# Hourglass attention and hypermixer: loading the values in half as many DMAs, and q and k by partition halves with crossed heads

## The chip, the cores and the metric

The kernel runs on one core of one Trainium2 chip. The metric is the device time of one execution in microseconds (us). A few executions are timed for each kernel, always beside executions of the kernel before on the same chip, and one is profiled. A run is called "slow" when it is more than 1.5% above the fastest of the same kernel, and the comparisons use the fast ones alone. The span that a profile shows is about 1 to 4 us shorter than the device time of the same run. Start times in the text are us from the start of the profiled span.

Short names: PE is TensorE, PEld its weight loads, DVE VectorE, ACT ScalarE, POOL GpSimd, SP the SyncE queue that issues the DMAs.

## The reference, cut to what matters

The inputs q, k and v are float32 of shape (8 batches, 8 heads, 576 rows, 64), drawn as 0.1 times a normal variate. Everything below is done for each batch.

```python
factor, Sd, scale = 4, 576 // 4, 1 / 8
# coarse attention on means of four rows, repeated four times
q_d, k_d, v_d = (t.reshape(B, H, Sd, 4, D).mean(axis=3) for t in (q, k, v))
out_up = np.repeat(sm_attn(q_d, k_d, v_d), 4, axis=2)
# local attention: a row sees the rows at a distance below 4
mask = np.abs(pos[:, None] - pos[None, :]) < 4
scores = np.where(mask, scale * q @ k.T, -1e9)
out_local = softmax(scores) @ v
x = (out_up + out_local)                       # then heads are put side by side: (B, 576, 512)
# token mixing
W_tok = (x @ w_q) @ (x @ w_k).T / 8
out = np.maximum(W_tok @ x, 0) @ w_out
```

## The kernel before

The batches are pipelined: while PE works on batch b, the data of batch b+1 are cast and those of b+2 are loaded. All loads are issued by SP in program order.

q and k of a batch arrive in one DMA each. Partition p receives 18 consecutive rows of heads 0 to 3 (u = 0) and 18 of heads 4 to 7 (u = 1), in runs of 18 x 64 x 4 = 4,608 bytes:

```python
def load_qk(b):
    for src, nm in ((q[b], "q32"), (k[b], "k32")):
        t = st[b][nm] = big.tile([128, 2, 18 * D], FP32, name=nm, tag="qk32", bufs=4)
        sp.dma_start(t, _ap(src, 0, [[18 * D, 128], [4 * S * D, 2], [1, 18 * D]]))
```

The values arrive as 64-row windows, one for each group of 58 queries: n counts five windows in each token half c. Partition half g holds every second head. A DMA brings four heads of one window, which is 256 runs of 256 bytes (64 KB), and a batch takes 20 of them. K0 is clamped at both ends of the sequence, so the two token halves don't always start 288 rows apart:

```python
K0 = [[min(max(Q0[n][c] - 3, 0), S - 64) for c in range(2)] for n in range(NW)]

def load_v(b):
    v32 = st[b]["v32"] = big.tile([128, NW, 2, 4, D], FP32, name="v32", tag="v32")
    for n in range(NW):
        for c in range(2):
            for g in range(2):
                sp.dma_start(v32[64 * g:64 * g + 64, n, c],
                             _ap(v[b], (g * S + K0[n][c]) * D, [[D, 64], [2 * S * D, 4], [1, D]]))
```

The casts to 16 bit: q and k of batch 0 on DVE and ACT, those of later batches on POOL; the values always on POOL, in one instruction for a batch.

```python
def qk():
    cast("q", dve.tensor_copy if b == 0 else pool.tensor_copy)
    cast("k", act.copy if b == 0 else pool.tensor_copy)
def vv():
    pool.tensor_copy(v16..., g_["v32"]...)
```

PE then transposes q and k (outputs `pq`, `pk`). Head group u becomes the partition half p of `qT` and `kT`. In the local scores p is the half that a matmul reads and g the half of the values' heads, to which it writes. All four combinations (p, g), the four quadrants of the array, are in use:

```python
for p, g in ((0, 0), (1, 1), (0, 1), (1, 0)):
    hl = 2 * y + g
    pe.matmul(p_[64 * g:64 * g + 64, p, o:o + w],
              kT[64 * p:64 * p + 64, hl, K0[n][c]:K0[n][c] + 64],
              qT[64 * p:64 * p + 64, hl, Q0[n][c]:Q0[n][c] + w], ...,
              tile_position=(64 * p, 64 * g))
```

The step `vd` (output `pv`) reduces the values for the coarse attention. It is the first work of a batch that needs the values, and its start is what this text calls the start of a batch. The order of issue around it, cut:

```python
ORDER = [ ... (0, "sums"), (1, "cast_qk"), (-1, "wt"), (0, "vd"), (0, "mask0"), (0, "score0"), (-1, "wks"),
          (2, "load_qk"), (1, "cast_v"), ..., (1, "tq"), (0, "ca0"), (2, "load_v"), ..., (1, "tk"), ... ]
```

The softmax here doesn't subtract the row's maximum and nothing guards it: scores larger than these inputs give would overflow.

## Time and profile before

The time was 225.13 us in both of two runs. The profiled run has a span of 223.8 us.

| what | number | where it is read |
|---|---|---|
| PE busy | 75% of the span, other engines at most 52% | busy table |
| wait of `pv` for the value cast | 14.3 us in two waits, 8.6 and 5.6 us | waits, timeline |
| wait of the value cast of batch 0, and of batch 1, for data | 16.1 and 12.0 us | waits |
| 20 value issues of batch 0 | 17.0 us | timeline |
| batch starts | 23.4, 46.7, 70.9, 94.5, 117.4, 142.9, 165.6, 187.7 us | timeline |

The first lines of the page of the kernel before: busy us with the share of the span and the number of instructions for each engine; then three rows of the view in 40 slices of 5.6 us, where a digit is tenths of a slice (9 is 90% or more; for PEclk tenths of the full TensorE clock).

```profile
PE 167.9 (75%) x2816; PEld 110.6 (49%) x2816; DVE 107.0 (48%) x260; ACT 99.1 (44%) x141; POOL 115.3 (52%) x112
...
PE   0060788267699779986996689978997799789680
...
PEclk9996558757889967997699959995899699958999
DMA  6946993597379349933998389836992474002206
```

From the ninth slice on PE is busy for 6 to 9 tenths of almost every slice; before that it has gaps (slices 1, 2, 4 and 8). The DMA row shows those engines only 3 to 6 tenths busy in slices 3, 4, 7 and 8, although values are being waited for.

Waits of the kernel before: engine and tile, what it waited for, us in total, times, longest.

```profile
POOL v L27 <- DMA v<-in_v_dram: 38.5, 7, 12.0
...
POOL v L27 <- DMA w<-in_moe_w_q_dram: 16.1, 1, 16.1
...
PE pv L27 <- POOL v L27: 14.3, 2, 8.6
```

The second line is really the last value DMA of batch 0, issued at 18.19 and landed at 20.80. The load of w_q shares its completion semaphore with an earlier value DMA of batch 0 (issued at 13.58), for which the cast waits as well; its updates begin at 21.01, just before the cast at 21.03, and the view names what came last.

The DMA part of the page: queue, number of DMAs, KB of one, median us from issue to landing.

```profile
v<-in_v_dram SPq DMA_DIRECT2D x160, 64.0 KB, 2.9
q<-in_q_dram SPq DMA_DIRECT2D x8, 1152.0 KB, 7.1
k<-in_k_dram SPq DMA_DIRECT2D x8, 1152.0 KB, 10.4
```

The timeline of the first 50 us: start, length, engine, line, instruction, output and input, count; in brackets, how long the engine had waited and for what.

```profile
1.80 17.00 SPq L27 DMA_DIRECT2D v<-in_v_dram  x20
...
3.18 1.28 ACT L27 ACT_TABLE_LOAD   x1 [3.18 <-POOL PB L80]
...
9.41 2.85 ACT L27 CAST k<-k 128x1152 f16<-128x1152 f32 x2 [4.95 <-DMA k<-in_k_dram]
...
17.54 1.03 DVE L27 TENSOR_TENSOR kd<-sum 128x160 f16<-128x160 f32 x4
...
21.03 2.32 POOL L27 CAST v<-v 128x2560 f16<-128x2560 f32 x1 [16.11 <-DMA w<-in_moe_w_q_dram]
...
23.40 0.85 PE L27 MATMUL pv<-v,Pm 64*32 64x260 f16 x24 [8.62 <-POOL v L27]
...
44.35 2.32 POOL L27 CAST v<-v 128x2560 f16<-128x2560 f32 x1 [11.98 <-DMA v<-in_v_dram]
...
46.73 0.85 PE L27 MATMUL pv<-v,Pm 64*32 64x260 f16 x24 [5.64 <-POOL v L27]
```

The first line is the key to the start of this kernel: 20 issues fill SP's queue from 1.80 to 18.80, and the value cast can only start when the last of them has landed.

Last, the stretch from the third batch start to the eighth, by the view of windows: stretch, its length, busy us of PE, PEld, DVE, ACT and POOL with counts, mean granted clock, DMA share, GB/s.

```profile
70.90:187.70 116.80, 101.65 (x1763) 67.23 (x1762) 60.58 (x128) 58.09 (x86) 76.90 (x68) 0.87 0.70 195
```

In this text the run is cut into "the start" (to the third batch start, 70.9 us here), "the steady stretch" (these 116.8 us) and the rest (36.1 us).

### The profile page before, as it was taken

Reading aid. Unit: us, or ns where it says so; the run is one execution under the profiler, and the core shown is the slowest. Engines: PE = TensorE matmul, PEld = TensorE weight load, DVE = VectorE, ACT = ScalarE, POOL = GpSimd, SP = SyncE. Lnnn points to the kernel's source line nnn. Section 1 sums busy time; section 2 is a strip of 40 time slices with the busy share of each in tenths; the row PEclk is TensorE's granted clock in tenths of the full one; section 3 lists DMA queues with packets and bytes.
Section 4 is the critical chain, followed back from the end, with each engine's and each line's share of the span. In section 5 each row is a group of like instructions: output and inputs, shape, how many; then the busy total and the mean of one; then the engine's idle time right before and its main releaser. Section 6 shows DMA issues by size and latency. Waiting matters only on the chain. (4 is left out here: it accounts for less than half of the span.)

```text
span 223.8 us, 6572 instructions
## 1 busy us (share of the span) xinstructions
PE 167.9 (75%) x2816; PEld 110.6 (49%) x2816; DVE 107.0 (48%) x260; ACT 99.1 (44%) x141; POOL 115.3 (52%) x112
## 2 busy tenths in 40 slices
PE   0060788267699779986996689978997799789680
PEld 0050467143476456653674367645764676446330
DVE  4813275215735663558243744565356545654230
ACT  2360456033556534465264254644464546433331
POOL 6002970099638954895459741994199359100000
PEclk9996558757889967997699959995899699958999
DMA  6946993597379349933998389836992474002206
GB/s 231 282 95 128 397 269 75 105 400 113 85 227 315 74 103 342 333 64 89 274 355 154 87 238 360 166 78 205 301 289 60 94 293 144 3 3 94 97 10 225
DMA packets 54572, 40.58 MB, mean 181 GB/s; under 512 B 45264, under 2 KB 45328, under 8 KB 54544
## 3 DMA queue, kind: packets, MB, share of 16 engines
q1 hardware_dynamic: 54464, 40.12, 62.5%
q8 instruction: 22, 0.36, 0.7%
q14 instruction: 6, 0.05, 0.1%
q10 hardware_dynamic: 80, 0.05, 0.1%
HBM read 30.67 MB, written 9.44 MB: 179 GB/s over the span
## 5 line engine op out<-in xcount | busy, mean ns | idle before, releaser
L27 POOL CAST v<-v 128x2560 f16<-128x2560 f32 x8 | 18.6, 2322 | 54.6 <-DMA v<-in_v_dram 38.5
L27 PE MATMUL po<-wo,rmx 128*128 128x512 f16 x128 | 36.1, 432 | 0.1
L27 ACT COPY os<-po 128x1024 f32<-128x1024 f32 x16 | 16.2, 1012 | 29.7 <-PE po L27 23.1
L27 DVE TENSOR_TENSOR x<-pav,rz 128x512 f16<-128x512 f32 x40 | 27.7, 691 | 1.4
L27 POOL TENSOR_TENSOR sum<-qT 128x1152 f32<-128x1152 f16 x8 | 16.8, 2106 | 18.2 <-ACT qT L27 17.8
L27 PE MATMUL pq<-id,q 128*128 128x128 f32 x64 | 15.6, 425 | 12.3 <-DVE q L27 10.7
L27 PEld LDWEIGHTS <-rmx 128*128 128x128 f16 x144 | 14.7, 109 | 17.2 <-issue 6.9
L27 ACT ACTIVATE E<-psc 128x928 f16<-128x928 f32 (+1 forms) x24 | 19.4, 806 | 6.4 <-PE psc L27 5.7
L27 PE MATMUL pmx<-wT,M 64*128 64x288 f16 x64 | 11.7, 318 | 11.9 <-DVE x L27 4.6
L27 POOL CAST q<-q 128x1152 f16<-128x1152 f32 x14 | 20.2, 1488 | 0.0
L27 POOL CAST k<-k 128x1152 f16<-128x1152 f32 x14 | 20.2, 1485 | 0.0
L27 PEld LDWEIGHTS pq<-id,q 128*128 128x128 f32 x64 | 12.5, 224 | 14.0 <-DVE q L27 10.7
L27 ACT ACTIVATE Ec<-pcs 128x1008 f16<-128x1008 f32 (+1 forms) x16 | 13.9, 874 | 11.2 <-PE pcs L27 11.2
L27 PE MATMUL pav<-v,E 64*64 64x65 f16 x640 | 14.1, 210 | 3.2 <-issue 2.1
L27 DVE RECIPROCAL rc<-pca 128x8 f32<-128x8 f32 (+1 forms) x16 | 3.2, 203 | 27.1 <-PE pca L27 27.1
L27 PE MATMUL pv<-v,Pm 64*32 64x260 f16 (+1 forms) x192 | 4.9, 286 | 14.3 <-POOL v L27 14.3
L27 POOL TENSOR_TENSOR sum<-kT 128x1152 f32<-128x1152 f16 x7 | 14.7, 2106 | 0.5
L27 PEld LDWEIGHTS <-E 64*64 64x64 f16 x640 | 9.7, 117 | 10.5 <-issue 7.9
L27 DVE RECIPROCAL rz<-pav 128x8 f32<-128x8 f32 x40 | 8.1, 203 | 14.0 <-PE pav L27 13.8
L27 PEld LDWEIGHTS <-Ec 128*128 128x128 f16 x160 | 12.4, 123 | 4.2 <-issue 0.8
L27 ACT COPY qT<-pq 128x1024 f32<-128x1024 f32 x8 | 8.1, 1012 | 13.5 <-PE pq L27 13.5
L27 DVE TENSOR_TENSOR vblk<-pv,blk 64x260 f16<-64x260 f32 x16 | 6.8, 427 | 14.1 <-ACT vd L27 14.0
(79 smaller groups left out, 327.9 us busy)
## 6 DMA issues: line engine op xcount, KB each, us to landing
v<-in_v_dram SPq DMA_DIRECT2D x160, 64.0 KB, 2.9
q<-in_q_dram SPq DMA_DIRECT2D x8, 1152.0 KB, 7.1
k<-in_k_dram SPq DMA_DIRECT2D x8, 1152.0 KB, 10.4
out_dram<-os SPq DMA_DIRECT2D x16, 512.0 KB, 3.1
wo<-in_moe_w_out_dram SPq DMA_DIRECT2D x2, 512.0 KB, 11.9
out_dram<-ol SPq DMA_DIRECT2D x8, 128.0 KB, 2.9
w<-in_moe_w_q_dram SPq DMA_DIRECT2D x1, 128.0 KB, 2.6
w<-in_moe_w_k_dram SPq DMA_DIRECT2D x1, 128.0 KB
```

Source lines behind the costliest of these rows:

```text
L27: return lambda *a, **k: self._tc.keep_in_program_order(f_(*a, **k))
```

## The change

Its intent is to load the values in 10 DMAs of 128 KB instead of 20 of 64 KB. One DMA shall carry four heads and both token halves. For that the halves g now hold heads 0 to 3 and 4 to 7, and K0 is no longer clamped, so that heads and token halves together are one uniform step of 288 rows: eight runs of rows, and a pattern of only three dimensions. (Taking both token halves in one DMA with the heads as they were needs a fourth dimension.) At the two ends of the whole tensor a DMA of 61 or 59 rows and a memset replace what is outside.

With g = heads 0 to 3 or 4 to 7 for the values and the same groups for q and k, only two of the four quadrants would be used. So the halves of q and k are crossed: for heads 2, 3, 6 and 7 the partition half is exchanged. That is done while loading. It needs a different destination for partitions 0 to 63 (heads 0, 1, 4, 5) and for 64 to 127 (heads 2, 3, 6, 7), so each of q and k becomes two DMAs of 64 partitions.

```diff
-    K0 = [[min(max(Q0[n][c] - 3, 0), S - 64) for c in range(2)] for n in range(NW)]
+    K0 = [[q0 - 3 for q0 in Q0[n]] for n in range(NW)]
 ...
     def load_qk(b):
-            sp.dma_start(t, _ap(src, 0, [[18 * D, 128], [4 * S * D, 2], [1, 18 * D]]))
+            for a in range(2):
+                w = 18 * D
+                sp.dma_start(_ap(t, 64 * a * row(t) + a * w, [[row(t), 64], [w - 2 * a * w, 2], [1, w]]),
+                             _ap(src, 2 * a * S * D, [[w, 64], [4 * S * D, 2], [1, w]]))
     def load_v(b):
-            for c in range(2):
-                for g in range(2):
-                    sp.dma_start(v32[64 * g:64 * g + 64, n, c],
-                                 _ap(v[b], (g * S + K0[n][c]) * D, [[D, 64], [2 * S * D, 4], [1, D]]))
+            for g in range(2):
+                o, lo, hi = (4 * g * S + K0[n][0]) * D, 0, 8
+                if (b, n, g) == (0, 0, 0):
+                    dve.memset(v32[0:3, 0, 0], 0.0)
+                    sp.dma_start(v32[3:64, 0, 0], _ap(v[b], 0, [[D, 61], [1, D]]))
+                    lo = 1
+                ... (the same at the other end, with 59 rows)
+                sp.dma_start(v32[64 * g:64 * g + 64, n, lo:hi],
+                             _ap(v[b], o + lo * HS * D, [[D, 64], [HS * D, hi - lo], [1, D]]))
 ... (masks, pooling weights, padding around kT, the order within the casts of q and k, and the order of heads follow)
     def score(pr_):
                             for p, g in ((0, 0), (1, 1), (0, 1), (1, 0)):
-                                hl = 2 * y + g
+                                hl = 2 * (p ^ g) + y
     def ca(i):
-                    pe.matmul(p_[:, p, 0:260], w_(p, 0, 2), vblk[:, p]...)
+                    for a in range(2):
+                        pe.matmul(p_[:, p ^ a, 130 * a:130 * a + 130], w_(p, 0, 2),
+                                  vblk[:, p ^ a, 2 * a:2 * a + 2]...)
     def m2():
-            dve.tensor_copy(M2[64:128], M2[0:64])
+            dve.tensor_copy(M2[64:128].bitcast(FP32), M2[0:64].bitcast(FP32))
```

More of the change, by code (lines that the diff above doesn't have):

```diff
@@ L94, in load_qk @@
             t = st[b][nm] = big.tile([128, 2, 18 * D], FP32, name=nm, tag="qk32", bufs=4)
-            sp.dma_start(t, _ap(src, 0, [[18 * D, 128], [4 * S * D, 2], [1, 18 * D]]))
+            for a in range(2):
+                w = 18 * D
+                sp.dma_start(_ap(t, 64 * a * row(t) + a * w, [[row(t), 64], [w - 2 * a * w, 2], [1, w]]),
+                             _ap(src, 2 * a * S * D, [[w, 64], [4 * S * D, 2], [1, w]]))
     def load_v(b):
-        v32 = st[b]["v32"] = big.tile([128, NW, 2, 4, D], FP32, name="v32", tag="v32")
+        v32 = st[b]["v32"] = big.tile([128, NW, 8, D], FP32, name="v32", tag="v32")
         for n in range(NW):
-            for c in range(2):
-                for g in range(2):
-                    sp.dma_start(v32[64 * g:64 * g + 64, n, c],
-                                 _ap(v[b], (g * S + K0[n][c]) * D, [[D, 64], [2 * S * D, 4], [1, D]]))
+            for g in range(2):
[4 more added lines that the diff above has]
+                    lo = 1
+                if (b, n, g) == (B - 1, NW - 1, 1):
+                    dve.memset(v32[96:128, n, 7], 0.0)
+                    sp.dma_start(v32[64:123, n, 7], _ap(v[b], o + 7 * HS * D, [[D, 59], [1, D]]))
+                    hi = 7
+                sp.dma_start(v32[64 * g:64 * g + 64, n, lo:hi],
+                             _ap(v[b], o + lo * HS * D, [[D, 64], [HS * D, hi - lo], [1, D]]))
     st = [{} for _ in range(B)]
@@ L127 @@
     nc.vector.memset(neg, 0.0)
-    for i0, i1, off, d in ((0, 2, -8, 5), (2, 3, 0, 0)):
-        t_ = neg[0:64, i0:i1]
-        asel(t_, [[-d, i1 - i0], [0, 2], [-1, 64]], ALU.is_ge, NEG, 3 - off, 1)
-        asel(t_, [[d, i1 - i0], [0, 2], [1, 64]], ALU.is_ge, NEG, off + 3, -1)
+    for cm, base in ((1, 6), (-1, 0)):
+        asel(neg[0:64], [[0, 3], [0, 2], [-cm, 64]], ALU.is_ge, NEG, base, cm)
+    asel(neg[0:64, 1], [[0, 2], [1, 64]], ALU.is_ge, NEG, -3, 0)
+    asel(neg[0:64, 2], [[0, 2], [-1, 64]], ALU.is_ge, NEG, 58, 0)
     nc.scalar.dma_start(neg[64:128], neg[0:64])
@@ L154 @@
     for i in range(NV):
-        t_ = cst.tile([128, NW, 2, 4, 65], FP16, name=f"v16_{i}")
-        nc.vector.memset(t_.rearrange("q n c h e -> q (n c h) e")[:, :, 64:65], 1.0)
+        t_ = cst.tile([128, NW, 4, 2, 65], FP16, name=f"v16_{i}")
+        nc.vector.memset(t_.rearrange("q n h c e -> q (n h c) e")[:, :, 64:65], 1.0)
         v16S.append(t_)
     RNG = [(0, 15), (1, 15), (1, 16), (2, 16), (2, 16)]
-    PB = cst.tile([128, NW + 2, 16], FP16, name="PB")
+    PB = cst.tile([128, NW, 16], FP16, name="PB")
     dve.memset(PB, 0.0)
-    for j, (lo, hi) in enumerate(RNG + [RNG[0], RNG[4]]):
+    for j, (lo, hi) in enumerate(RNG):
         dve.memset(PB[:, j, lo:hi], 0.25)
     for g in range(2):
-        for j0, j1, base, d in ((0, NW, -3, 2), (NW, NW + 2, 0, 0)):
-            u_ = PB[64 * g:64 * g + 64, j0:j1]
-            asel(u_, [[d, j1 - j0], [-4, 16]], ALU.is_ge, 0.0, base, 1)
-            asel(u_, [[-d, j1 - j0], [4, 16]], ALU.is_ge, 0.0, 3 - base, -1)
+        u_ = PB[64 * g:64 * g + 64]
+        asel(u_, [[2, NW], [-4, 16]], ALU.is_ge, 0.0, -3, 1)
+        asel(u_, [[-2, NW], [4, 16]], ALU.is_ge, 0.0, 6, -1)
     Pm = cst.tile([128, NW, 2, 32], FP16, name="Pm")
     dve.memset(Pm, 0.0)
-    dve.tensor_copy(Pm[:, 1:5, 0, 0:16], PB[:, 1:5])
-    dve.tensor_copy(Pm[:, 0:4, 1, 16:32], PB[:, 0:4])
-    dve.tensor_copy(Pm[:, 0, 0, 0:16], PB[:, NW])
-    dve.tensor_copy(Pm[:, 4, 1, 16:32], PB[:, NW + 1])
+    for c in range(2):
+        dve.tensor_copy(Pm[:, :, c, 16 * c:16 * c + 16], PB)
     blk = cst.tile([128, 2], FP16, name="blk")
@@ L183 @@
         dve.memset(rows[64 * c:64 * c + 58], 1.0)
+    kTS = []
+    for i in range(2):
+        t_ = cst.tile([128, 9 * 128 + 6], FP32, name=f"kT_{i}")
+        dve.memset(t_[:, 0:2], 0.0)
+        dve.memset(t_[:, 9 * 128 + 2:], 0.0)
+        kTS.append(t_)
     vd0S, vblkS, wTS, wkS, M2S, od1S = [], [], [], [], [], []
@@ L232, in cast @@
             for u in range(2):
-                f_(_ap(d_, 2 * D * u, [[row(d_), 128], [4 * D, 9], [1, 2], [2, D]]),
-                   s_[:, u].rearrange("p (f s e) -> p f s e", s=2, e=D))
+                f_(_ap(d_, 2 * D * u, [[row(d_), 128], [1, 2], [4 * D, 9], [2, D]]),
+                   s_[:, u].rearrange("p (f s e) -> p s f e", s=2, e=D))
         def qk():
@@ L241, in vv @@
             v16 = g_["v16"] = v16S[b % NV]
-            pool.tensor_copy(v16.rearrange("q n c h e -> q (n c h) e")[:, :, 0:64],
-                             g_["v32"].rearrange("q n c h e -> q (n c h) e"))
+            pool.tensor_copy(v16.rearrange("q n h c e -> q (n h c) e")[:, :, 0:64],
+                             g_["v32"].rearrange("q n x e -> q (n x) e"))
         return {"cast_qk": qk, "cast_v": vv}
@@ L256, in f_ @@
                                  t_[:, f].rearrange("p u e s -> p (u e s)"), id32)
-                t_ = g_[dst] = big.tile([128, 128, 9], FP32, name=dst, tag=dst)
+                if dst == "kT":
+                    t_ = kTS[b % 2][:, 2:2 + 9 * 128].rearrange("p (t f) -> p t f", f=9)
+                else:
+                    t_ = big.tile([128, 128, 9], FP32, name=dst, tag=dst)
+                g_[dst] = t_
                 evac(dst, t_[:, :, 0:8], p_.rearrange("p a (f t) -> p t (a f)", f=4))
@@ L275, in sums @@
                               **(dict(tag="xT") if i == 1 and b == 0 else dict(tag="sum2", bufs=1)))
-                t4 = t_.bitcast(FP16).rearrange("p a f -> p (a f)").rearrange("p (t f) -> p t f", f=4)
+                t4 = t_.rearrange("p a f -> p (a f)").bitcast(FP16).rearrange("p (t f) -> p t f", f=4)
                 add(s_, t4[:, :, 0:2], t4[:, :, 2:4], op=ALU.add)
@@ L294, in f_ @@
                 N = 4 * len(pr_)
-                parts = {(0, 3): ((0, 2, 2), (2, 8, 1)), (1, 2): ((0, 8, 1),),
-                         (4,): ((0, 2, 1), (2, 4, 0))}[pr_]
+                parts = {(0, 3): ((0, 2, 1), (2, 8, 0)), (1, 2): ((0, 8, 0),),
+                         (4,): ((0, 2, 0), (2, 4, 2))}[pr_]
                 for lo, hi, ty in parts:
@@ L307, in f_ @@
             def f_():
-                qT, kT = (g_[x].bitcast(FP16).rearrange("p (h t) f -> p h (t f)", h=4)
-                          for x in ("qT", "kT"))
+                qT = g_["qT"].rearrange("p a f -> p (a f)").bitcast(FP16)
+                kT = kTS[b % 2].bitcast(FP16)
                 p_ = g_["psc", pr_]
@@ L315, in f_ @@
                             for p, g in ((0, 0), (1, 1), (0, 1), (1, 0)):
-                                hl = 2 * y + g
+                                hl = 2 * (p ^ g) + y
                                 o = ((i * 2 + c) * 2 + y) * w
+                                ok, oq = S * hl + K0[n][c] + 4, S * hl + Q0[n][c]
                                 pe.matmul(p_[64 * g:64 * g + 64, p, o:o + w],
-                                          kT[64 * p:64 * p + 64, hl, K0[n][c]:K0[n][c] + 64],
-                                          qT[64 * p:64 * p + 64, hl, Q0[n][c]:Q0[n][c] + w],
+                                          kT[64 * p:64 * p + 64, ok:ok + 64],
+                                          qT[64 * p:64 * p + 64, oq:oq + w],
                                           start=False, stop=True, skip_group_check=True,
@@ L336, in vd @@
                         pe.matmul(pv[32 * n:32 * n + 32, g, 0:260], Pm[64 * g:64 * g + 64, n, c],
-                                  v16[64 * g:64 * g + 64, n, c].rearrange("q h e -> q (h e)"),
+                                  v16[64 * g:64 * g + 64, n, :, c, :],
                                   start=(c == 0), stop=(c == 1), skip_group_check=True,
@@ L340, in vd @@
             for c in range(2):
-                for y in range(2):
+                for hl in range(4):
                     for g in range(2):
-                        o = 32 * (2 * g + y)
-                        pe.matmul(pv[o:o + 32, g, 260:390], Pm[64 * g:64 * g + 64, 4, c],
-                                  v16[64 * g:64 * g + 64, 4, c].rearrange("q (p y) e -> q y p e", y=2)[:, y],
+                        pe.matmul(pv[32 * hl:32 * hl + 32, g, 260:325], Pm[64 * g:64 * g + 64, 4, c],
+                                  v16[64 * g:64 * g + 64, 4, hl, c, :],
                                   start=(c == 0), stop=(c == 1), skip_group_check=True,
-                                  tile_position=(64 * g, o))
+                                  tile_position=(64 * g, 32 * hl))
             evac("vd0", vd0.rearrange("q g h e -> q g (h e)"), pv[:, :, 0:260])
-            for g in range(2):
-                lo = 64 * g
+            for a in range(2):
+                lo = 64 * a
                 dve.tensor_tensor(
-                    _ap(vblk, lo * row(vblk) + 65 * g, [[row(vblk), 64], [260, 2], [130, 2], [1, 65]]),
-                    _ap(pv, lo * row(pv) + 512 * g + 260, [[row(pv), 64], [65, 2], [0, 2], [1, 65]]),
+                    _ap(vblk, lo * row(vblk) + 130 * a, [[row(vblk), 64], [260, 2], [65, 2], [1, 65]]),
+                    _ap(pv, lo * row(pv) + 260, [[row(pv), 64], [512, 2], [0, 2], [1, 65]]),
                     _ap(blk, lo * row(blk), [[row(blk), 64], [0, 2], [1, 2], [0, 65]]),
@@ L379, in f_ @@
                 for hl in range(4 if i == 0 else 0):
-                    o = 32 * (2 * (hl % 2) + hl // 2)
+                    o = 32 * hl
                     for p in range(2):
@@ L403, in f_ @@
                 for p in range(2):
-                    pe.matmul(p_[:, p, 0:260], w_(p, 0, 2), vblk[:, p].rearrange("a h e -> a (h e)"),
-                              start=True, stop=False, skip_group_check=True)
+                    for a in range(2):
+                        pe.matmul(p_[:, p ^ a, 130 * a:130 * a + 130], w_(p, 0, 2),
+                                  vblk[:, p ^ a, 2 * a:2 * a + 2].rearrange("q h e -> q (h e)"),
+                                  start=(p == 0), stop=False, skip_group_check=True)
+                for p in range(2):
                     for hl in range(4):
-                        pe.matmul(p_[:, p, 65 * hl:65 * hl + 65], w_(p, hl // 2, hl % 2),
-                                  vd0[:, hl % 2, 2 * p + hl // 2, :],
-                                  start=False, stop=(hl == 3), skip_group_check=True)
+                        g = p ^ (hl // 2)
+                        pe.matmul(p_[:, g, 65 * hl:65 * hl + 65], w_(p, hl // 2, hl % 2), vd0[:, g, hl, :],
+                                  start=False, stop=True, skip_group_check=True)
                 n = 40 if i else 128
@@ L436, in f_ @@
                 p_ = ps(name="pav")
-                for hq in range(4):
+                for hl in range(4):
                     for g, c in ((0, 0), (1, 1), (0, 1), (1, 0)):
-                        pe.matmul(p_[64 * c:64 * c + 64, g, 65 * hq:65 * hq + 65],
-                                  E[64 * g:64 * g + 64, hq // 2, i, c, hq % 2, :],
-                                  v16[64 * g:64 * g + 64, n, c, hq, :],
+                        pe.matmul(p_[64 * c:64 * c + 64, g, 65 * hl:65 * hl + 65],
+                                  E[64 * g:64 * g + 64, g ^ (hl // 2), i, c, hl % 2, :],
+                                  v16[64 * g:64 * g + 64, n, hl, c, :],
                                   start=True, stop=True, tile_position=(64 * g, 64 * c))
@@ L445, in f_ @@
                 dve.tensor_tensor(
-                    x_.rearrange("p (h g e) -> p g h e", g=2, h=4),
+                    x_.rearrange("p (g h e) -> p g h e", g=2, h=4),
                     _ap(p_, 0, [[row(p_), 128], [512, 2], [65, 4], [1, 64]]),
```

## The prediction

> **What bounds it now.** The busy table gives PE 75% of the span, no other engine over 52%; PE is 82-89% busy from 55 to 180 us, and batches start (first pv matmul, timeline) every 22-26 us. The loss is at the start: PE waits 8.6 us for the cast of batch 0's values (14.8 to 23.4) and 5.6 us for batch 1's (41.1 to 46.7). Both casts wait for their DMA (16.1 and 12.0 us, view of waits), and the granted clock is 0.5 from 18.6 to 35.7 and 42.5 to 52.7. Later value casts end 3-9 us before PE needs them.
>
> Those loads are issue bound: 20 issues of 64 KB, one per 0.66 us, only ~100 GB/s; packets of 256 B take 18 ns. Also only eight DMAs are in flight: the seventh and eighth value issues start when q and k land.
>
> **What the change does.**
> 1. Values: 10 issues of 128 KB per batch instead of 20, same 5,120 packets. The 512-run weight load issues in 0.5-0.6 us, so issue cost should not grow: about 7 us per batch instead of 13. Then packets limit: when loads pile up (8-10 and 50-52 us) 256 B packets take 30 ns and the stream gives 170-205 GB/s: about 7 us.
> 2. q and k: each 128-partition load becomes two of 64. [...] 2 KB packets of the 64-partition stores of ol, where alone, take a median 151 ns, those of the 128-partition os 84. So 4,608 B packets should go from 180 to about 340 ns, q plus k of a batch from 5.8 to about 10.9 us (512 x 340 ns / 16, an estimate).
> 3. Up to batch 1's values the stream is estimated at 2.3 + 10.9 + 7.3 + 1.2 (w) + 10.9 + 2.6 (wo) + 7.3 + 0.8 = 43.2 us; before, that cast starts at 44.35. So what the issues give, the halves take back: batch 0's values land about as now (20-22 us), batch 1's 0-3 us earlier. k(0) lands near 13.5-14 instead of 9.4, within PE's slack of 8.6 us.
> 4. PE: 96 more matmuls and weight loads (vblk 2x130 columns for 260, 65 for 130), nearly the same columns. pca runs at column rate (30 ns per 65 warm), so 0.1 us per batch, up to 1 us in all.
> 5. The M copy as 32 bit (286 to 1,257 ns): no change assumed. q's first cast and the mask setup may get faster, off the path.
>
> **On the critical path**: -0 to -4 us at the start, +0.3 to +1 us of PE. Steady batches keep their spacing: DMA work of about 21 us per batch still fits.
>
> **Predicted 224.8 us, 219.5 to 229.0; faster by over 2%: 0.20, within 2%: 0.70, slower: 0.10.**
>
> **Signs.** Right: 10 value issues per batch of about 0.6 us each; 4,608 B packets near 340 ns; k(0) landing after 13 us; first pv within 1.5 us of 23.4, second at 43-47; later spacing unchanged. Wrong: packets still near 180 ns; then the start shrinks by about 11 us, to 214.
>
> **What could make it wrong.** [...] Slower q and k may make POOL's casts late in steady batches and reach PE's transposes (slower).

The sum in step 3 came to 43.2 us, with 10.9 twice for q and k. The 10.9 rests on my estimate of "about 340 ns"; the two stores that step 2 names, 151 and 84 ns, would by their ratio give 324 (180 x 151 / 84, an estimate).

## The result, and the profile after

The changed kernel took 231.45 us (231.38 and 231.52), and the kernel before 225.13. The ratio is 1.028, with a 95% interval from 1.024 to 1.033: slower by 2.8%. A ratio here is the mean time of one kernel's fast runs over that of the other's of the same rounds, so it is not quite the ratio of the medians. A repeat in a later session gave 231.78 against 225.47, ratio 1.026 [1.015, 1.037]; by itself its interval is too wide to call it slower by over 2%.

The page of the changed kernel (span 229.3 us), the same lines:

```profile
PE 167.4 (73%) x2912; PEld 112.3 (49%) x2912; DVE 113.3 (49%) x262; ACT 99.4 (43%) x141; POOL 115.7 (50%) x108
...
PE   0024357764699959995999499968996799779680
...
PEclk9999999999569985999599959995899679979998
DMA  5999999799999999999999999999980004202205
```

PE's busy time is unchanged although it runs 96 more matmuls. What has changed is the DMA row: it is full from the second slice to the last load. (The nines of the PEclk row before its first other digit are no measurement: the clock record of this trace starts at 42.9 us, that of the kernel before at 15.2.) Its waits, its DMAs and its timeline:

```profile
POOL v L27 <- DMA w<-in_moe_w_k_dram: 18.2, 1, 18.2
...
ACT L27 <- DMA k<-in_k_dram: 15.3, 1, 15.3
...
POOL v L27 <- DMA v<-in_v_dram: 12.1, 2, 7.8
...
PE pv L27 <- POOL v L27: 6.6, 2, 5.0
```

```profile
v<-in_v_dram SPq DMA_DIRECT2D x78, 128.0 KB, 4.9
q<-in_q_dram SPq DMA_DIRECT2D x16, 576.0 KB, 9.0
k<-in_k_dram SPq DMA_DIRECT2D x16, 576.0 KB, 11.3
```

```profile
3.58 15.34 SPq L27 DMA_DIRECT2D v<-in_v_dram  x11
...
15.33 1.28 ACT L27 ACT_TABLE_LOAD   x1 [15.33 <-DMA k<-in_k_dram]
16.62 2.79 ACT L27 CAST k<-k 128x1152 f16<-128x1152 f32 x2
...
23.49 3.28 POOL L27 CAST v<-v 128x2560 f16<-128x2560 f32 x1 [18.21 <-DMA w<-in_moe_w_k_dram]
...
24.62 5.92 DVE L27 TENSOR_TENSOR kd<-sum 128x160 f16<-128x160 f32 x4
26.82 0.74 PE L27 MATMUL pv<-v,Pm 64*32 64x260 f16 x32 [4.95 <-POOL v L27]
...
46.98 2.33 POOL L27 CAST v<-v 128x2560 f16<-128x2560 f32 x1 [7.75 <-DMA v<-in_v_dram]
...
49.36 0.48 PE L27 MATMUL pv<-v,Pm 64*32 64x260 f16 x32 [1.68 <-POOL v L27]
```

The wait of `pv` for the cast is less than half of what it was, and yet `pv` starts later, at 26.82 instead of 23.40 and at 49.36 instead of 46.73. That is no contradiction. The end of the wait is set by the cast, and both casts start later (23.49 against 21.03, 46.98 against 44.35), because their data land later. The wait is shorter only because PE arrives later: k of batch 0 lands at 15.3 instead of 9.4, and so its transposes, which come before `pv`, are late as well. Eleven value issues still keep SP busy for 15.34 us, because their number is not what holds them now. Here the second to the fifth of them take 2.0 to 3.9 us each while q and k move, until 14.1 us, and the last six about 0.7. In e5 below, where the DMA of 61 rows is cut, no value issue of batch 0 takes more than 0.7 us, but three of them start at 6.42, 9.17 and 11.93, just when the q or k DMA eight places before has landed (6.41, 9.15, 11.91): in these traces eight completion semaphores take turns, and an issue waits for the DMA eight before. The kernel before shows it too: its sixth and seventh value issues start at 6.10 and 9.41, and the DMAs of q and k, whose semaphores they wait for (eight before, with the one DMA that ACT issues), landed at 6.08 and 9.39. Either way the half-rate q and k hold the issues up, and the last value issue starts at 18.26 here and at 18.43 there. In this trace the data are later still: that last DMA lands 5.1 us after its issue, at 23.34.

The median record of a 4,608-byte packet is 178 ns in the kernel before and 355 ns in this one. That is a factor of two (1.99).

The steady stretch by the view of windows:

```profile
74.70:193.80 119.10, 103.24 (x1831) 68.64 (x1831) 63.09 (x129) 58.27 (x86) 76.29 (x68) 0.86 0.90 193
```

The 5.5 us between the two profiles' spans divide thus, from the batch starts: start 74.7 - 70.9 = +3.8, steady stretch 119.0 - 116.8 = +2.2, rest 35.5 - 36.1 = -0.6.

### The profile page after: what moved, and what is told of

Same layout as the page of the kernel before. It is cut to its first block, busy times and chain, and to the rows that moved or that the text cites. A ratio compares the mean times of both kernels' runs of the same rounds, so it can differ in the third digit from the quotient of the medians.

```text
span 229.3 us, 6708 instructions
## 1 busy us (share of the span) xinstructions
PE 167.4 (73%) x2912; PEld 112.3 (49%) x2912; DVE 113.3 (49%) x262; ACT 99.4 (43%) x141; POOL 115.7 (50%) x108
## 5 line engine op out<-in xcount | busy, mean ns | idle before, releaser
L27 PE MATMUL po<-wo,rmx 128*128 128x512 f16 x128 | 36.9, 440 | 0.1
L27 POOL CAST v<-v 128x2560 f16<-128x2560 f32 x8 | 19.5, 2442 | 30.4 <-DMA w<-in_moe_w_k_dram 18.2
L27 ACT COPY os<-po 128x1024 f32<-128x1024 f32 x16 | 16.2, 1014 | 30.8 <-PE po L27 19.5
L27 PE MATMUL pq<-id,q 128*128 128x128 f32 x64 | 15.6, 425 | 12.4 <-DVE q L27 10.9
L27 PE MATMUL pmx<-wT,M 64*128 64x288 f16 x64 | 11.6, 330 | 11.5 <-ACT E L27 3.9
L27 PEld LDWEIGHTS pq<-id,q 128*128 128x128 f32 x64 | 12.5, 224 | 14.2 <-DVE q L27 10.9
L27 PEld LDWEIGHTS <-E 64*64 64x64 f16 x640 | 10.2, 121 | 14.7 <-issue 11.8
L27 DVE RECIPROCAL rz<-pav 128x8 f32<-128x8 f32 x40 | 8.2, 205 | 16.5 <-PE pav L27 16.3
L27 PE MATMUL pk<-id,k 128*128 128x128 f32 x64 | 10.3, 313 | 6.8 <-ACT k L27 6.6
L27 PEld LDWEIGHTS <-Ec 128*128 128x128 f16 x192 | 13.6, 122 | 2.5 <-issue 0.4
L27 DVE COPY kT<-pr 128x128 f32<-128x128 f32 x8 | 3.1, 391 | 23.0 <-ACT qT L27 23.0
```

Source lines behind the costliest of these rows:

```text
L27: return lambda *a, **k: self._tc.keep_in_program_order(f_(*a, **k))
```

## The experiments

Theory A: fewer value issues are a large gain by themselves, and loading q and k by partition halves, at half the packet rate, takes all of it and more. Rival B: the compute edits (crossed heads, 96 more matmuls, the 32-bit copy of M) cost the time, and the loads are nearly neutral, as the prediction had it. Rival C: it is the larger number of q and k issues, not their partitions. Rival D: small side effects at the start, that is the 61-row DMA or the late table load.

All ratios are against the kernel before, on the same chip and in the same rounds. The experiments ran on four chips, so kernels are best compared by their ratios. Three kernels (marked "heads wrong") lose the crossing, so that for half of the heads the values of one head meet q and k of another. They are for the time only. The comparison with the reference still called them correct, because with inputs of 0.1 the attention weights are almost uniform: the reference itself, recomputed off the chip with those heads exchanged, moves by only 0.01 relative, but by 0.80 when q and k are twelve times and v three times as large.

| run | q, k loads | value issues | us, median | ratio [95%] |
|---|---|---|---|---|
| changed kernel | 2 x 64 partitions, halves | 10 | 231.45 | 1.028 [1.024, 1.033] |
| e0 (the same again) | halves | 10 | 231.78 | 1.026 [1.015, 1.037] |
| e1 (heads wrong) | 1 x 128 | 10 | 209.84 | 0.934 [0.926, 0.941] |
| e4 (heads wrong) | 2 x 128 partitions | 10 | 212.78 | 0.946 [0.933, 0.958] |
| e8 | 2 x 64, even and odd | 10 | 214.42 | 0.949 [0.939, 0.958] |
| e14 (heads wrong) | 1 x 128 | 20 | 226.53 | 1.005 [1.000, 1.010] |
| e11 | even and odd | 20 | 229.51 | 1.017 [1.010, 1.025] |
| e2 (kernel before) | halves | 20 | 252.16 | 1.123 [1.114, 1.132] |

### e1: q and k whole again, the rest of the change kept

```diff
-            for a in range(2): ...      # two DMAs of 64 partitions
+            sp.dma_start(t, _ap(src, 0, [[18 * D, 128], [4 * S * D, 2], [1, 18 * D]]))
```

> The changed kernel with the whole, 128-partition loads of q and k of the kernel before, nothing else (values come out wrong on purpose: heads are no longer crossed). Theory (64-partition loads run at half rate[...]): 4,608 B packets back to 180 ns, k(0) lands near 9.5 us instead of 15.3, first pv near 18-19.5 us, second at 35-38, no idle of PE before it; 213 to 217 us. Rival (the 96 extra matmuls and the other compute edits cost the 6 us): stays at 229-232.

It took 209.84 us, ratio 0.934. One edit of the loads alone is worth 22 us, so B is out as the main cause.

### e2: the kernel before with q and k by halves (no crossing)

```diff
-            sp.dma_start(t, _ap(src, 0, [[18 * D, 128], [4 * S * D, 2], [1, 18 * D]]))
+            for a in range(2):
+                sp.dma_start(t[64 * a:64 * a + 64],
+                             _ap(src, 2 * a * S * D, [[18 * D, 64], [4 * S * D, 2], [1, 18 * D]]))
```

> The kernel before with each load of q and k split into two of 64 partitions, nothing else (right results). Theory (half rate): 4,608 B packets at 340-370 ns, k(0) lands after 13.5 us, and as its values still take 20 issues behind that, batch 1's cast starts at 47-53 instead of 44.35; 229 to 235 us. Rival (compute edits): 224-227.

It took 252.16 us, ratio 1.123: the direction that A gives, but far more than I expected. The median 4,608-byte packet was 358 ns. The batch starts are 23.8 to 28.3 us apart all along, and the steady stretch is 130.9 us. Twenty issues of 0.66 us (13 us) and q and k at half rate (11.5 us, an estimate: 512 x 358 ns / 16) together are more than the 23 us of a batch. In the trace PE waits for the value cast in six of the eight batches (17.9 us in all), where it was two before, so here the loads reach later batches and not only the start.

### e4: q and k in two DMAs each as in the changed kernel, but each over 128 partitions

```diff
             for a in range(2):
-                sp.dma_start(_ap(t, 64 * a * row(t) + a * w, [[row(t), 64], [w - 2 * a * w, 2], [1, w]]), ...)
+                sp.dma_start(t[:, a], _ap(src, 4 * a * S * D, [[18 * D, 128], [1, 18 * D]]))
```

> The changed kernel with q and k still in two issues each, but split along u, so that each spans 128 partitions (wrong values on purpose). It keeps the number of issues, the eight in flight and the two waits of the k cast (the activation table load stays behind one of them). Theory[...]: like e1_whole_qk within 2 us, packets near 180 ns. Rival (the extra issues and waits cost it): like the changed kernel, 229-232.

It took 212.78 us, ratio 0.946, with packets of 178 ns. C is out as the main cause: two DMAs over all partitions cost at most a little against one (the intervals of e1 and e4 overlap), while the same number over half the partitions each, in the changed kernel, costs 19 us more than e4. It is the partitions.

### w: whole q and k, no crossing, scores on two quadrants (heads right)

```diff
-                            for p, g in ((0, 0), (1, 1), (0, 1), (1, 0)):
-                                hl = 2 * (p ^ g) + y
+                            for j, p in ((0, 0), (0, 1), (1, 0), (1, 1)):
+                                hl = 2 * j + y
...
-                                          tile_position=(64 * p, 64 * g))
+                                          tile_position=(64 * p, 64 * p))
```

> A right version: whole loads of q and k, values by halves of the heads in 10 issues, heads not crossed, so scores use two quadrants of the PE array instead of four; vblk by one matmul of 260 columns as before. Theory: the start as in e1_whole_qk; scores cost 0.3 to 0.8 us more per batch; 215 to 221 us, so faster than both kernels. If four quadrants are what the speed rests on: 224 or more.

It took 218.61 us, ratio 0.972 [0.965, 0.979]. So giving up the four quadrants and keeping the whole load already beats both kernels. Against e1 it is 8.8 us slower, and PE is busy for 170.1 us instead of 161.0: this is what the crossing buys, although part of it is clock (30.7 us at half clock against 23.9, see below). The crossing was worth having; the way of loading it was not.

### e8: crossed heads by even and odd partitions (heads right)

Two DMAs over a half of the partitions each take 355 ns for a packet (the changed kernel), two over all of them 178 (e4). That 64 partitions spread over all of them keep the 178 ns was my supposition; no trace had shown it before this run. So the two DMAs go to even and odd partitions instead of the lower and the upper half, and the rows come back into order without another instruction, in the access pattern with which the transposes are taken out of PSUM:

```diff
-                sp.dma_start(_ap(t, 64 * a * row(t) + a * w, [[row(t), 64], [w - 2 * a * w, 2], [1, w]]),
+                sp.dma_start(_ap(t, a * row(t) + a * w, [[2 * row(t), 64], [w - 2 * a * w, 2], [1, w]]),
...
-                evac(dst, t_[:, :, 0:8], p_.rearrange("p a (f t) -> p t (a f)", f=4))
+                evac(dst, t_[:, :, 0:8].rearrange("p (h j) f -> p h j f", h=2),
+                     p_.rearrange("p a (f j h) -> p h j (a f)", f=4, h=2))
...
-                evac("r" + nm, g_[nm + "T"][:, :, 8], pr[:, 128 * i:128 * i + 128])
+                evac("r" + nm, g_[nm + "T"][:, :, 8].rearrange("p (h j) -> p h j", h=2),
+                     pr[:, 128 * i:128 * i + 128].rearrange("p (j h) -> p h j", h=2))
```

> The changed kernel, right results, same number and size of DMAs and still 64 partitions in each, but one load of a pair takes the even and the other the odd partitions of q and k[...]; the copies out of PSUM put the columns back in order. Theory[...]: 4,608 B packets near 180 ns, k(0) lands near 9.5 us, 210 to 215 us. Rival (any load of 64 partitions is slow, or four issues): packets near 350 ns, 229 to 233 us.

It took 214.42 us, ratio 0.949, with all outputs right. Packets are back at 178 ns. From its DMA part, its timeline and its steady stretch (columns as above):

```profile
q<-in_q_dram SPq DMA_DIRECT2D x16, 576.0 KB, 5.4
k<-in_k_dram SPq DMA_DIRECT2D x16, 576.0 KB, 7.3
```

```profile
18.82 2.59 POOL L27 CAST v<-v 128x2560 f16<-128x2560 f32 x1 [13.55 <-DMA w<-in_moe_w_k_dram]
...
21.46 0.74 PE L27 MATMUL pv<-v,Pm 64*32 64x260 f16 x32 [4.95 <-POOL v L27]
...
36.61 2.32 POOL L27 CAST v<-v 128x2560 f16<-128x2560 f32 x1 [5.94 <-DMA v<-in_v_dram]
...
40.64 0.48 PE L27 MATMUL pv<-v,Pm 64*32 64x260 f16 x32
```

```profile
63.85:174.20 110.35, 97.92 (x1823) 67.09 (x1822) 60.69 (x129) 58.13 (x86) 76.11 (x68) 0.89 0.70 195
```

The bytes, the number of DMAs and the matmuls are those of the changed kernel. The second `pv` no longer waits for its cast, and the whole kernel is 17 us faster than the changed one. This settles A: which partitions a DMA spans is the loss. It is also the best right kernel found, and it was run again below.

### e5: the 61-row DMA as 48 and 13 rows

I suspected that the DMA of 61 rows lags and so held back batch 0's values. In the trace of the changed kernel its completion semaphore gets a single update when its data land (15.90 us), that of the 48 rows in e5 gets sixteen (15.17 to 15.49). I read this as one DMA engine instead of sixteen, which is not shown: the trace does not name a packet's engine.

```diff
-                    sp.dma_start(v32[3:64, 0, 0], _ap(v[b], 0, [[D, 61], [1, D]]))
+                    sp.dma_start(v32[3:51, 0, 0], _ap(v[b], 0, [[D, 48], [1, D]]))
+                    sp.dma_start(v32[51:64, 0, 0], _ap(v[b], 48 * D, [[D, 13], [1, D]]))
```

> The changed kernel with its first load of values, 61 rows, as 48 and 13 rows, nothing else. Theory: [...] without it the last values of batch 0 land 1.3 to 2 us earlier (cast from 23.5 to about 21.5-22.2), batch 1's 0.5-2 us earlier; 229 to 231 us. Rival (no lag): cast stays at 23.3-23.7, 231-232 us.

It took 232.22 us, ratio 1.030 [1.023, 1.038]: no gain, a miss of mine; the rival that I had named holds. The cast starts no earlier than the 23.49 of the changed kernel:

```profile
23.66 3.02 POOL L27 CAST v<-v 128x2560 f16<-128x2560 f32 x1 [18.39 <-DMA v<-in_v_dram]
```

### e7 and e7b: the activation table loaded early

In the changed kernel the cast of k(0) waits for two DMAs, and one of the two waits has come to stand before the table load, which runs at 15.33 instead of 3.18. One Exp of one column was put first on ACT.

```diff
+    warm = cst.tile([128, 1], FP32, name="warm")
+    dve.memset(warm, 0.0)
+    act.activation(warm, warm, ACTF.Exp)
```

> The changed kernel with a one-column activation put first on ACT, so that the activation table is loaded at the start and not behind the wait for the second half of k. Expected: the cast of k starts near 15.4 instead of 16.6 us and pk 1.2 us earlier; DVE's sums of batch 0 collide less with POOL's cast of values; first pv 0-1 us earlier; but the second pv waits for its DMA as before, so 230.3 to 231.8 us.

> e7_table_early again: on another chip it lay 1.1% above the kernel before where the changed kernel lay 2.6-2.8% above. If that gain is real: ratio 1.005 to 1.018. If it was luck of the clock windows: 1.02 to 1.035.

They took 228.13 and 228.68 us, ratios 1.011 [1.003, 1.020] and 1.012 [1.007, 1.017]: a real gain of about 3 us on the changed kernel. The load moved, as e7's timeline shows:

```profile
5.83 1.28 ACT L27 ACT_TABLE_LOAD   x1 [5.83 <-DVE rows L27]
...
25.40 0.74 PE L27 MATMUL pv<-v,Pm 64*32 64x260 f16 x32 [4.95 <-POOL v L27]
```

But the start of e7 is only 0.4 us shorter (74.3 against 74.7); 2.4 us of the gain are in the steady stretch (116.6 against 119.0). And with the loads put right (e9 below) it is worth nothing. So it is no fixed price of the table load.

### e10: the M copy in 16 bit

```diff
-            dve.tensor_copy(M2[64:128].bitcast(FP32), M2[0:64].bitcast(FP32))
+            dve.tensor_copy(M2[64:128], M2[0:64])
```

> e8_even_odd with the copy of M in 16 bit as in the kernel before, nothing else. Expected: copy times of 286 ns undisturbed and 0.4-1.2 us beside POOL in both, no difference beyond 1%: 210 to 215 us. If the 32-bit form helps or hurts, the ratio of the two tells.

On top of e8 it took 215.68 us, ratio 0.957 [0.951, 0.963], against 0.949 [0.939, 0.958] for e8. The intervals overlap; if the 32-bit copy gains anything, it is at most about 1%.

### e14: the compute edits alone

Whole q and k, and the values in 20 issues in the new layout.

```diff
-            for a in range(2): ...      # two DMAs of 64 partitions
+            sp.dma_start(t, _ap(src, 0, [[18 * D, 128], [4 * S * D, 2], [1, 18 * D]]))
...
-                sp.dma_start(v32[64 * g:64 * g + 64, n, lo:hi], ...)
+                for l_, h_ in ((lo, 4), (4, hi)):
+                    sp.dma_start(v32[64 * g:64 * g + 64, n, l_:h_], ...)
```

> The changed kernel with the loads of the kernel before: q and k whole, values in 20 issues (head crossing lost, so wrong values on purpose). What is left of the change is its compute: 96 more matmuls, the casts' order, the M copy in 32 bit. If the compute edits cost the 4 us by which e11_v_20_issues lay above the kernel before: 228-231 us. If the two more issues per batch and the second wait of the k cast cost them: 224-227 us, and k's table load back before the data.

It took 226.53 us, ratio 1.005 [1.000, 1.010]. The compute edits cost about 1 us (at most 1%), so B is no more than a small part.

### e11: e8 with the values in 20 issues

The edit is the second half of the one above, on e8.

> e8_even_odd with the values of a batch in 20 issues of 64 KB again, nothing else: [...] compute edits as in the changed kernel. Theory (the gain of e8_even_odd is the halved issues alone): back to the kernel before, 222 to 228 us, second pv at 44-48 us. Rival (the compute edits gain too): under 220.

It took 229.51 us, ratio 1.017 [1.010, 1.025]: with nothing else changed, ten issues more cost 15 us against e8. The first two value casts are as late as in the changed kernel:

```profile
24.36 2.32 POOL L27 CAST v<-v 128x2560 f16<-128x2560 f32 x1 [19.10 <-DMA w<-in_moe_w_q_dram]
...
47.54 2.32 POOL L27 CAST v<-v 128x2560 f16<-128x2560 f32 x1 [11.86 <-DMA v<-in_v_dram]
```

### e12 and e13: halves only in later batches, only in batches 0 and 1

e12 loads batches 0 and 1 by even and odd partitions and the later ones by halves; e13 does the opposite.

```diff
+                eo = b < 2                 # e13: b >= 2
-                sp.dma_start(_ap(t, a * row(t) + a * w, [[2 * row(t), 64], ...
+                sp.dma_start(_ap(t, (1 if eo else 64) * a * row(t) + a * w, [[(2 if eo else 1) * row(t), 64], ...
```

> Even and odd partitions for batches 0 and 1, partition halves from batch 2 on (right results): the start as in e8_even_odd, the steady batches as in the changed kernel. My prediction's claim that steady batches keep their spacing means 213 to 216 us. The traces so far (pv 2 to pv 7: 119.0 us in the changed kernel, 110.4 in e8_even_odd) mean 219 to 224.

> The reverse: halves for batches 0 and 1, even and odd partitions later (right results). If the start alone costs, as the changed kernel, 228-232. By the traces the start costs 10-13 us and the steady batches 8: 221 to 226 us; together with e12_halves_later the two losses should add up to that of the changed kernel over e8_even_odd, about 17 us.

e12 took 219.69 us, ratio 0.971 [0.961, 0.980], and e13 225.46, ratio 1.000 [0.992, 1.008]. Over e8, which ran on another chip, these are 5.3 and 11.0 us (2.2% and 5.1% by the ratios), together 16.3, where the changed kernel loses 17.4 (231.78 of the repeat less 214.42). So about two thirds of the loss come from the first two batches. The steady stretch of e12 is almost as short as that of e8, although its DMA share shows the half-rate loads at work:

```profile
67.80:179.40 111.60, 98.64 (x1823) 67.54 (x1822) 60.74 (x129) 58.04 (x86) 76.13 (x68) 0.89 0.94 199
```

### e8b and e9: the best version again, and with the early table load

> e8_even_odd again, as the partner of the next: 212 to 216 us, ratio 0.94 to 0.957.

> e8_even_odd with the early table load of e7. The k cast starts 1.2 us earlier (near 10 instead of 11.2 us), but the first pv waits for the values' cast all the same; 0 to 2 us less than e8b_even_odd, so 211 to 215 us.

e9 is e8 with the three lines of e7. e8b took 215.46 us, ratio 0.948 [0.941, 0.954], and e9 213.32, ratio 0.946 [0.942, 0.950]: the same.

### e0: the changed kernel again

> The changed kernel once more, as the partner of the three others of this call on the same chip: 230 to 233 us, ratio to the kernel before 1.02 to 1.035.

231.78 us, ratio 1.026. The steady stretch is 119.3 us (119.0 in the first profile), so its length is not chance of one run.

### The steady stretch and the clock

The halves do not directly explain why the changed kernel is slower in the steady stretch, as e12 shows. What goes with its length (the two lowest rows are level) is the time in it for which the clock was granted at half, read from the clock record of each trace (e2, where loads hold up later batches too, has 44.4 us and 130.9):

| kernels | us at half clock in the steady stretch | its length, us |
|---|---|---|
| e1, e4, e8, e10, e12 | 23.9 | 110.4 to 111.6 |
| e13 | 27.3 | 113.5 |
| before, e7, e14, w | 30.7 | 116.6 to 117.2 |
| changed kernel, its repeat | 34.1 | 119.0 to 119.3 |
| e5, e11 | 37.5 | 118.7 to 119.6 |

The steps are 3.4 us. In the clock records of the kernel before and of the changed one, all stretches at one clock but the last take 3.41, 6.83, 10.24, 13.65, 17.07 or 20.48 us. From 83.88 to 179.45 us the stretches at half clock of the changed kernel start 23.9 us apart, seven such steps; its batches are about 23.8 us apart, and those of e8 about 22.1. PE's gaps over 0.1 us in the stretch add up to 15.0 us before and 15.6 in the changed kernel. PE's busy time in it grew by 1.6 us (101.65 to 103.24), about what 3.4 us more at half speed would cost (1.7, an estimate; the 128x512 matmuls of `po` start 216 ns apart at full clock and 427 at half, in the median, in both traces). So the extra 2.2 us are mostly half-clock time, and not waiting for data. Against e8 the stretch is 8.7 us longer: 5.3 of them are PE's busy time, the rest gaps. How a kernel falls into its rhythm, no run settles. That the start decides is the reading that fits e12 (halves only later: 111.6 us) and e13 (halves only at the start: 113.5); it is not shown beyond these.

## Why the prediction was wrong

It said 224.8 us, within 219.5 to 229.0, and "within 2%" at 0.70. The measured 231.45 us lies above the range, and the kernel is slower by 2.8%.

**What held.** Value issues were 10 per batch (11 in batch 0) at 0.6 to 0.7 us each for twice the bytes, as said, where q and k did not hold them. The half-rate packets were 355 ns (said: near 340). k of batch 0 landed after 13 us, at 15.3. The compute edits cost about 1 us (e14, +0.5%). The M copy made no difference that e10 could see. The mechanism, that the halves take back what the issues give, was right in kind: 15 us given (e11 to e8) and 17 us taken (e8 to the changed kernel). (A slip: the value issues that waited for q and k before were the sixth and seventh, at 6.10 and 9.41, not "the seventh and eighth".)

**The step that failed is step 3, the balance "what the issues give, the halves take back": without the halves the change gives less at the start than its sum counted.** By the sum, "43.2 us", batch 1's cast would start "0-3 us earlier" than 44.35; it started at 46.98. With the full-rate 5.8 us of step 2 in place of both 10.9 the same sum gives 33.0. So it counted a gain of about 11 us by the rest of the change against a loss of 10.2 us by the halves. e8 splits the two, because its cast of batch 1 starts at 36.61. The loss by the halves, from 36.61 to 46.98, is 10.4 us, as said. But the gain by the rest, from 44.35 to 36.61, is 7.7 us instead of 11 (8.3 in e1, with q and k whole, where the cast starts at 36.07). The ten fewer issues alone do give 10.9 us, from e11 to e8, but e11, with its two more issues for q and k, starts from 47.54 and not from 44.35.

Which terms were short shows from landing to landing (a DMA has landed with the last update of its semaphore in the trace). All in us; in brackets where the term ends:

| term of the sum | said | changed kernel | e8 (said with 5.8) |
|---|---|---|---|
| q and k of batch 0, from 2.3 | 10.9 | 13.0 (15.3) | 7.6 (9.9) |
| values of batch 0 | 7.3 | 8.1 (23.3) | 8.8 (18.7) |
| w | 1.2 | 1.9 (25.2) | 0.8 (19.5) |
| q and k of batch 1 | 10.9 | 11.0 (36.2) | 5.7 (25.2) |
| wo | 2.6 | 3.7 (40.0) | 4.8 (30.0) |
| values of batch 1 | 7.3 | 6.9 (46.9) | 6.5 (36.5) |
| to the cast | 0.8 | 0.1 (47.0) | 0.1 (36.6) |

So the values of batch 0 landed at 23.3 and not at "20-22 us". The first q and k (+2.1), the values of batch 0 (+0.8) and wo (+1.1) took longer than said, and so they did in e8 (+1.8, +1.5, +2.2), where q and k move at full rate. The sums are 3.8 and 3.6 us short, so the halves are not the reason. Of the first 2.1 us, 1.2 lie between the last packet of k (14.09) and its landing (15.26), which this term leaves out, and about 0.5 are the packets' 355 ns instead of 340 (an estimate: 512 x 15 ns / 16). Why the other terms are longer, no run settles.

**The sign "first pv within 1.5 of 23.4" failed with it: it came at 26.82.** Of these 3.4 us, 2.5 are the later start of the cast just named. The other 1.0 us is the cast itself, 3.28 us instead of 2.32, and it goes back to k(0), whose lateness I had read as lying "within PE's slack of 8.6 us". That slack was counted for PE's wait alone. Behind k's landing came the table load (15.33) and the cast of k (16.62 instead of 9.41), and so the `kd` sums of DVE, before done at 18.6, now met POOL's value cast; there they took 5.92 us instead of 1.03. The same sums take 5.91 us in e5, e7 and e8, which have the overlap too, and 1.03 in e11, where they run before the cast. So it goes with the overlap; what slows both was not tested. e8 has this overlap and is fast all the same. The table load's part of the start is at most the 0.4 us of e7.

**"Steady batches keep their spacing" failed twice.** It went from 116.8 to 119.0 us in the changed kernel, with 34.1 us at half clock instead of 30.7. And with the partitions put right it would have fallen to 110.4. DMA work does fit into a batch, as I said (e12: 0.94 busy and 111.6 us), but the spacing was not given by PE's work alone: it went with the time at half clock (34.1 us for 119.0, 23.9 for 110.4).

**That 214 us came out for full-rate packets is partly luck.** The prediction names "about 11 us, to 214" as the sign of being wrong, and e8, where the packets are at 178 ns, took 214.4. But its start is shorter by 7.1 us (70.9 to 63.85), not 11. Another 6.4 us come from the steady stretch, which was to stay as it was. In a chain of runs: the kernel before at 1.000; compute edits, 1.005 (e14); two more q and k issues in a batch, and the late table load, 1.017 (e11); ten value issues instead of twenty, 0.949 (e8); q and k by halves instead of even and odd partitions, 1.026 to 1.028 (the changed kernel).

**What stays open.** Why e11 is about 3 us slower than e14 is clear only in part. Its cast of batch 1 starts 2.8 us later (47.54 against 44.78), and up to there it has four more issues for q and k; at 0.65 us each, on a queue that hardly pauses, they would be 2.6 us (an estimate). But at the third batch start only 1.1 us of it is left, and another 1.7 lie in the steady stretch, with 37.5 us at half clock instead of 30.7. What sets the clock rhythm of the steady stretch is open. So is a stall of PE of 4.13 us in the changed kernel, in which it waits for nothing that the profile names:

```profile
58.20 0.43 PE L27 MATMUL pav<-v,E 64*64 64x65 f16 x16 [4.13 <-issue]
```

It ends 1.3 us after a 16 KB packet of the instruction queue ended (56.93). The longest stall of the steady stretch ends 1.4 to 1.7 us after such a packet as well, in this trace (81.31 after 79.59), in that of e11 (169.72 after 168.25) and in that of the kernel before (122.64 after 121.28). But e8 has as many such packets (22), and no stall of its steady stretch exceeds 1 us. So this is a coincidence in time that no run tested.

## What to carry to other kernels

When a DMA is cut in two so that its parts can have different layouts, ask which partitions each part spans before counting issues or bytes: cutting into even and odd partitions kept 178 ns per packet, cutting into lower and upper halves made it 355, and that turned a gain of 5% into a loss of 3%. When you add up the loads of a queue, count each from landing to landing of the ones before and check the sum on a kernel that you have already measured: here it was 3.6 to 3.8 us short at batch 1's cast, at the full rate of q and k and at half of it alike. And check a gain that you expect from the start of a pipeline by the steady stretch too: here it moved there by 2.2 us with the time at half clock (30.7 us before, 34.1 in the changed kernel), while PE's gaps hardly changed (15.0 and 15.6 us).
